# The values products of an attention head: second parts first, and all twenty in one run on TensorE

## The chip, the cores and the metric

The kernel runs on one core of one Trainium2 chip. The metric is the device time of one execution in microseconds; a kernel's time is the median of several. Work is spread over five engines, each with its own queue that is worked through in order: TensorE (PE in the profile, its weight loads PEld), VectorE (DVE), ScalarE (ACT), GpSimd (POOL) and SyncE (SP, whose queue SPq issues the transfers here).

## What is computed

A block of adaptive layer norm, attention with a compressive memory, and a token-mixing MLP, on 2048 rows of 1024 numbers. The part that matters is the attention of one head in one segment of 512 rows; there are 32 heads and 4 segments, so 128 of them:

```python
logits = jnp.einsum("bhqd,bhkd->bhqk", qs, ks) * scale + mask
p = _softmax(logits, axis=-1)
a_dot = jnp.einsum("bhqk,bhkd->bhqd", p, vs)
...
o = g * a_mem + (1.0 - g) * a_dot
```

The mask is causal. `a_mem` comes from a memory that is carried from segment to segment. After the attention follow the output projection `o @ wo`, a second layer norm and the MLP.

## The kernel before

**Stages.** First the input is normed and projected (`project(0, ...)` and what stands around it, to about 140 us of the span). Then a loop over n works through the 128 heads, numbered t*4+h, where t counts 32 steps of four heads of one group and segment. After it come the output projection (`out_proj`, sixteen blocks of 128 rows) and the MLP (`mix`, to the end).

**One pass of the loop.** Pass n traces, in this order: `scores` of head n, `maxima` of head n+3 (`LEADS`), `values` of head n-1 (`VL` = 1), and then one of the four pieces of `project` that lies 8 heads ahead (`LEADP`). Into some passes go loads of normed rows (`reload_h`), of weights (`load_w`, and for the output projection lines 503 on), and of modulation weights (`mod_late`).

**scores** (lines 372 to 393) makes the unnormalised probabilities. Four products of q and k (lines 379, 382, 385, 386) go to two PSUM banks ("s2"), ACT takes their exponentials into `p32` (lines 380, 383, 387), POOL zeroes what the mask hides in the diagonal blocks (line 390, two instructions), ACT casts the result to float16 as the first part of `ph` (line 392), and POOL subtracts to get the rest as its second part (line 393). `p32` and `ph` have two buffers each.

**values** (lines 395 to 425) multiplies the probabilities with the values. For each of the two parts of `ph` there are ten products, one for each pair of a block i of 128 query rows and a block j of keys that the mask lets through. They differ in width: products of the first part have 97 columns (a column of ones for the softmax sum, then three parts of the values), those of the second part 65. All twenty add up in one PSUM bank, `pv`, of which there is one. Then DVE takes a reciprocal (line 410), a sum over the three parts (line 412) and a scaling (line 414); POOL adds the memory's share (line 417), and after the fourth head of a step the result is transposed on TensorE (line 422), copied (line 424) and stored to `oT` (line 425), from where `out_proj` loads it (line 553, tile `otr`).

**Order.** The program is traced as above, and a planner that builds each engine's queue (`schedule_with_timeline_sim=True`) takes, at each point of its own simulated time, among the instructions that are ready the one with the best priority; unless told otherwise, that is the one traced first. A queue once built is fixed: the engine then waits at each instruction for what it needs. `tc.high_priority()` puts what is traced inside it ahead of the rest among the ready ones. Products that add up in one bank stay in traced order among themselves.

Of the kernel before, what the change touches and what calls it, by code (L numbers as in the profile page):

```python
# [27 lines left out]
NV = 97  # L28
# [14 lines left out]
def attention_and_mlp(ctx, tc, x, wq, wkv, wo, beta, w1, b1, w2, b2, c, wm_a, wm_b, out):  # L43
    nc = tc.nc
    V, A, G, T, SY = nc.vector, nc.scalar, nc.gpsimd, nc.tensor, nc.sync
# [20 lines left out]
    def bank(tag, bufs, name):  # L66
        return psum.tile([P, 512], F32, tag=tag, bufs=bufs, name=name)
# [327 lines left out]
    def values(t, h):  # L395
        pr, g, seg = its[t]
        d = st[t]
        am, ph = d["am"], d["ph", h]
        pv = bank("pv", 1, f"pv{t}_{h}").rearrange("p (a n) -> p a n", a=4)
        col = {0: lambda i: 128 * i, 1: lambda i: 512 + 128 * (i - 1), 2: lambda i: 1024 + 128 * (i - 2),  # L400
               3: lambda i: 896}
        n = 0
        for part, w in ((0, NV), (1, 65)):
            for i in range(4):
                for j in range(i + 1):
                    o = col[j](i)
                    T.matmul(pv[:, i, 0:w], ph[:, part, o:o + 128], d["vp"][:, j, h, 0:w], start=(n == 0),  # L407
                             stop=(n == 19), skip_group_check=True)
                    n += 1
        V.reciprocal(pv[:, :, 0], pv[:, :, 0])  # L410
        red = r_.tile([P, 4, 32], F32, tag="red", bufs=2, name=f"red{t}_{h}")
        V.tensor_reduce(red, pv[:, :, 1:97].rearrange("p a (c e) -> p a e c", c=3), axis=AX.X, op=ALU.add)
        ah = am[:, :, 32 * h:32 * h + 32]
        V.scalar_tensor_tensor(red if seg else ah, red, gate[:, 1, 4 * g + h:4 * g + h + 1],
                               pv[:, :, 0:1].to_broadcast([P, 4, 32]), op0=ALU.mult, op1=ALU.mult)
        if seg:
            G.tensor_tensor(ah, ah, red, op=ALU.add)
        if h < 3:
            return
        ps = bank("ms", 1, f"ops{t}")  # L420
        for i in range(4):
            T.transpose(ps[:, 128 * i:128 * i + 128], am[:, i], ident)
        ot = r_.tile([P, L], F32, tag="ot", bufs=1, name=f"ot{t}")
        A.copy(ot, ps)
        SY.dma_start(oT[g, :, L * seg:L * seg + L], ot)
        del st[t]
# [52 lines left out]
    for n in range(-LEADS, 4 * NI + VL):  # L479
        at(scores, n)  # L480
        at(maxima, n + LEADS)
        at(values, n - VL)
        m = n + LEADP
        if 0 <= m + 4 < 4 * NI:
            t = (m + 4) // 4
            if its[t][:2] not in W:
                W[its[t][:2]] = load_w(its[t][1], its[t][0])
        if m >= 8:
            at(project, m)
        if 59 <= m < 67:  # L490
            seg, ct = 2 + (m - 59) // 4, 2 * ((m - 59) % 4)
            reload_h(seg, ct)
            reload_h(seg, ct + 1)
        if m == 4 * NI - 6:
            gaw = a.tile([P, D], F32, name="gaw")
            spread(gaw, 0)
        if 4 * NI - 4 <= m < 4 * NI + 4:
            i = m - 4 * NI + 4
            nh, c2 = i // 4, 2 * (i % 4)
            r = a.tile([P, 2, 512], F32, tag="raw", bufs=2, name=f"wor{i}")  # L500
            SY.dma_start(r, wo[P * c2:P * c2 + 2 * P, 512 * nh:512 * nh + 512].rearrange("(c p) n -> p c n", p=P))
            for j in range(2):
                V.tensor_tensor(r[:, j], r[:, j], gaw[:, 512 * nh:512 * nh + 512], op=ALU.mult)
                wop[c2 + j, nh] = new_page(f"wo{c2 + j}_{nh}")
                split(wop[c2 + j, nh], r[:, j], A, V)
        if n >= ML0 and (n - ML0) % MLS == 0 and (n - ML0) // MLS < 32:
            mod_late((n - ML0) // MLS)
# [10 lines left out]
    w = cw_pool.__enter__()  # L518
# [344 lines left out]
```

## Time and profile before

| | us |
|---|---|
| median of 3 runs | 2363.02 |
| lowest and highest | 2362.68, 2367.99 |
| the profiled execution | 2363.29 |
| its span (first to last instruction) | 2361.6 |

| stage of the span | from, to us | PE busy | DVE busy | ACT busy | POOL busy |
|---|---|---|---|---|---|
| loop, start | 140 to 200 | 52.49 of 60 | 31.35 | 37.28 | 25.76 |
| loop, first half | 200 to 620 | 394.10 of 420 | 310.76 | 246.67 | 243.76 |
| loop, second half | 620 to 1016 | 395.26 of 396 | 249.42 | 248.28 | 220.01 |
| loop, last projections | 1016 to 1062 | 35.91 of 46 | 40.75 | 26.81 | 26.74 |
| loop, no projections left | 1062 to 1104 | 22.40 of 42 | 9.50 | 19.07 | 23.11 |
| output projection and MLP | 1104 to 2361 | 1246.90 of 1257 | 992.54 | 443.71 | 98.17 |

How to read the profile: it is one execution. A row of the timeline gives the start of a run of like instructions, the time from the start of the first to the end of the last, the engine, the line, the operation, the tiles written and read, the count, and in brackets how long the engine had been idle and what ended that. Products on TensorE are pipelined: one lasts 0.2 to 0.4 us, but the next starts long before it ends, so what a product costs is the distance from its start to the next one's. A row of groups ends with the time that the group kept its engine busy, the mean time of one in ns, and the idle time ahead of it.

### The profile page before, as it was taken

The page shows a single profiled execution, that of the slowest core. Times are in us where ns is not written, and L with a number is a line of the kernel's source. Part 1 is how long each engine was busy: PE and PEld are TensorE (multiplying, and loading weights), DVE is VectorE, ACT ScalarE, POOL GpSimd, SP SyncE. Part 2 cuts the span into 40 slices and gives each one's busy share as a digit, 9 for nine tenths or more (in the row PEclk, how much of TensorE's full clock was granted, in tenths as well). Part 3 has the DMA queues.
Part 4 walks back from the last instruction along what each step waited for, and adds up shares of the span by engine and source line. Part 5 has one row for each costly group of instructions (what it writes and reads, how often), then busy time and mean ns, then how long its engine had stood idle before and what let it go on. Part 6 is the DMA issues. An engine that isn't in the chain of part 4 may idle for free.

```text
span 2361.6 us, 37994 instructions
## 1 busy us (share of the span) xinstructions
PE 2230.0 (94%) x13729; PEld 1914.9 (81%) x13729; DVE 1729.5 (73%) x3889; ACT 1091.7 (46%) x1959; POOL 679.7 (29%) x667
## 2 busy tenths in 40 slices
PE   1889999998999999986999999999999999999999
PEld 1778889887899999964887888888888888888887
DVE  7655777777766665692999665598889877878787
ACT  3556656555566666663333433353334232424232
POOL 2415546557655555553000000013333000000000
PEclk9889999999999999986999999999999999999999
DMA  9563555567544444451455665366557532424234
GB/s 316 178 208 94 171 153 171 162 205 234 174 118 118 122 118 127 117 171 46 136 195 199 248 256 196 125 251 246 211 201 264 208 120 82 135 66 138 67 108 151
DMA packets 152779, 390.00 MB, mean 165 GB/s; under 512 B 17776, under 2 KB 55696, under 8 KB 143632
## 3 DMA queue, kind: packets, MB, share of 16 engines
q1 hardware_dynamic: 152592, 387.58, 50.5%
q8 instruction: 109, 1.79, 0.3%
q14 instruction: 78, 0.64, 0.1%
HBM read 224.18 MB, written 112.48 MB: 143 GB/s over the span
## 4 chain that ended last, share of the span: by engine, by line
PE 75%; DMA 10%; DVE 9%; issue 2%; ACT 2%; POOL 1%; SPq 1%; DVEq 0%; ACTq 0%; POOLq 0%
PE mx L661 36%; PE nps L270 12%; PE po L568 7%; PE qps L295 7%; PE pv L407 3%; DMA xb<-x1d 2%; DMA x1e<-xb 2%; PE a L379 1%; PE sx L357 1%; PE sz L357 1%; DMA rawv<-in_wkv_dram 1%; DMA sk<-nt 1%; DVE bU L115 1%; PE rd L329 1%; DVE xb L714 1%
## 5 line engine op out<-in xcount | busy, mean ns | idle before, releaser
L661 PE MATMUL mx<-bU,sp 128*128 128x512 f32 x2352 | 535.7, 390 | 3.8 <-DVE sp L115 1.7
L661 PEld LDWEIGHTS mx<-bU,sp 128*128 128x128 f32 x2352 | 441.0, 188 | 98.0 <-DVE sp L115 2.7
L270 PE MATMUL nps<-wv,h 128*128 128x256 f32 x3072 | 443.9, 285 | 2.9 <-POOL h L115 1.5
L661 PE MATMUL mx<-bA,sp 128*128 128x512 f32 x1764 | 432.2, 390 | 2.2 <-ACT cc L666 0.9
L112 ACT CAST sp<-wr 128x384 fp32r<-128x384 f32 (+2 forms) x408 | 217.2, 545 | 445.1 <-PE mx L661 374.2
L270 PEld LDWEIGHTS nps<-wv,h 128*128 128x128 f32 x3072 | 408.2, 190 | 7.4 <-POOL h L115 2.0
L661 PEld LDWEIGHTS mx<-bA,sp 128*128 128x128 f32 x1764 | 330.8, 188 | 72.8 <-ACT cc L666 1.5
L393 POOL TENSOR_TENSOR ph<-p,ph 128x1280 f16<-128x1280 f32 x128 | 343.0, 2680 | 137.5 <-ACT ph L392 137.2
L115 DVE TENSOR_TENSOR sp<-wr,sp 128x384 fp32r<-128x384 f32 (+2 forms) x408 | 259.1, 646 | 32.3 <-ACT sp L112 32.2
L668 DVE TENSOR_TENSOR ac<-mx,ac 128x512 f32<-128x512 f32 x280 | 189.5, 686 | 91.8 <-PE mx L661 91.2
L295 PE MATMUL qps<-h,wq 128*128 128x512 f32 x768 | 197.8, 408 | 2.0 <-DVE r L280 2.0
L392 ACT CAST ph<-p 128x1280 f16<-128x1280 f32 x128 | 161.0, 1258 | 57.2 <-POOL p L390 56.7
L358 DVE CUSTOM_DVE_ANT_0 sx<-sx,mask 128x128 f32<-128x128 f32 (+1 forms) x256 | 109.7, 429 | 99.4 <-PE sx L357 97.2
L568 PE MATMUL po<-wo,ots 128*128 128x512 f32 x768 | 177.0, 394 | 5.7 <-ACT ots L112 5.7
L390 POOL TENSOR_SCALAR_AFFINE_SELECT p<-p 128x256 f32<-128x256 f32 x256 | 122.5, 487 | 185.8 <-ACT p L383 89.5
L568 PEld LDWEIGHTS po<-wo,ots 128*128 128x128 f32 x768 | 146.0, 190 | 36.7 <-ACT ots L112 6.1
L295 PEld LDWEIGHTS qps<-h,wq 128*128 128x128 f32 x768 | 145.0, 194 | 35.3 <-issue 1.7
L407 PE MATMUL pv<-vp,ph 128*128 128x97 bf16 (+1 forms) x2560 | 152.7, 209 | 13.8 <-POOL ph L393 7.5
L661 PE MATMUL mx<-bB,sp 128*128 128x512 f32 x588 | 164.4, 389 | 0.0
L407 PEld LDWEIGHTS <-ph 128*128 128x128 f16 x2560 | 120.8, 102 | 41.1 <-issue 12.5
L661 PEld LDWEIGHTS mx<-bB,sp 128*128 128x128 f32 x588 | 110.4, 188 | 22.9
L668 DVE TENSOR_TENSOR cc<-mx,cc 128x512 f32<-128x512 f32 x140 | 94.6, 683 | 45.4 <-PE mx L661 43.2
(163 smaller groups left out, 3175.8 us busy)
## 6 DMA issues: line engine op xcount, KB each, us to landing
sk<-sg SPq DMA_DIRECT2D x384, 128.0 KB
wr<-in_w_dram SPq DMA_DIRECT2D x28, 1024.0 KB
wr<-in_w_dram SPq DMA_DIRECT2D x32, 768.0 KB
bstu<-ucd SPq DMA_DIRECT2D x28, 768.0 KB
x<-in_x_dram SPq DMA_DIRECT2D x32, 512.0 KB
wsp<-wv SPq DMA_DIRECT2D x32, 512.0 KB
rawm<-in_wm_b_dram SPq DMA_DIRECT2D x32, 512.0 KB
wv<-wsp SPq DMA_DIRECT2D x32, 512.0 KB
```

What stands on the lines that cost most here:

```text
L112: A.copy(hi, src)
L115: lo_eng.tensor_tensor(lo, src, hi.bitcast(F32), op=ALU.subtract)
L270: T.matmul(ps[:, aa], hp[k][:, j, 128 * tt:128 * tt + 128], wt[:, i, o:o + 256], start=(n == 0), stop=(n >= 6 * NK - 2), skip_group_check= ...
L295: T.matmul(ps, wt[:, i, o:o + 128], hp[k][:, j], start=(n == 0), stop=(n == 3 * NK - 1))
L358: V.tensor_tensor_reduce(o, o, mask[:, 384 - 128 * i:], 1.0, -3.0e38, op0=ALU.add, op1=ALU.max, accum_out=mx[:, h % 2, i:i + 1])
L390: G.affine_select(w, w, pattern=[[0, 2], [1, 128]], compare_op=ALU.is_ge, fill=0.0, base=0, channel_multiplier=-1)
L392: A.copy(ph[:, 0], p32)
L393: G.tensor_tensor(ph[:, 1], p32, ph[:, 0], op=ALU.subtract)
L407: T.matmul(pv[:, i, 0:w], ph[:, part, o:o + 128], d["vp"][:, j, h, 0:w], start=(n == 0), stop=(n == 19), skip_group_check=True)
L568: T.matmul(ps, os_[:, i, P * ct:P * ct + P], wop[ct, nh][:, j], start=(n == 0), stop=(n == 3 * NK - 1))
L661: T.matmul(ps, ops[q][:, i, P * k:P * k + P], b[:, j], start=(m == 0 and first), stop=(m == 3 * nk - 1), skip_group_check=True)
L668: V.tensor_tensor(d, ps, d, op=ALU.add)
```

## The change

In `values`, the loop over the parts runs over the second part (65 columns) first, then the first (97 columns), and the twenty products are traced at high priority. The product with `start` is now the first of the second part. Nothing else differs.

```diff
-        for part, w in ((0, NV), (1, 65)):
-            for i in range(4):
-                for j in range(i + 1):
-                    o = col[j](i)
-                    T.matmul(pv[:, i, 0:w], ph[:, part, o:o + 128], d["vp"][:, j, h, 0:w], start=(n == 0),
-                             stop=(n == 19), skip_group_check=True)
-                    n += 1
+        with tc.high_priority():
+            for part, w in ((1, 65), (0, NV)):
+                for i in range(4):
+                    for j in range(i + 1):
+                        o = col[j](i)
+                        T.matmul(pv[:, i, 0:w], ph[:, part, o:o + 128], d["vp"][:, j, h, 0:w], start=(n == 0),
+                                 stop=(n == 19), skip_group_check=True)
+                        n += 1
```

## The prediction

> **What bounds the kernel now.** I read the page first, then the stages of the loop, then TensorE's own order inside them. On the page TensorE is the busiest engine; the rows of weight loads are used below.
>
> ```profile
> span 2361.6 us, 37994 instructions
> ...
> PE 2230.0 (94%) x13729; PEld 1914.9 (81%) x13729; DVE 1729.5 (73%) x3889; ACT 1091.7 (46%) x1959; POOL 679.7 (29%) x667
> ...
> L270 PEld LDWEIGHTS nps<-wv,h 128*128 128x128 f32 x3072 | 408.2, 190 | 7.4 <-POOL h L115 2.0
> ...
> L407 PEld LDWEIGHTS <-ph 128*128 128x128 f16 x2560 | 120.8, 102 | 41.1 <-issue 12.5
> ```
>
> The profiled execution took 2363.29 us, 1.7 more than its span, and the median of the runs is 2363.02; I sum against the execution, which is the median within 0.3 us. The stages of the loop follow (busy us of PE, PEld, DVE, ACT, POOL with their counts, then the clock, DMA share and GB/s).
>
> ```profile
> 200.00:400.00 200.00, 193.17 (x1721) 177.89 (x1721) 146.11 (x420) 126.19 (x228) 109.18 (x110) 0.98 0.55 161
> 400.00:620.00 220.00, 200.93 (x1689) 180.91 (x1687) 164.65 (x451) 120.48 (x212) 134.58 (x121) 0.95 0.64 191
> 620.00:1016.00 396.00, 395.26 (x3535) 364.22 (x3534) 249.42 (x841) 248.28 (x440) 220.01 (x248) 1.00 0.45 123
> 1062.00:1104.00 42.00, 22.40 (x159) 15.24 (x155) 9.50 (x26) 19.07 (x28) 23.11 (x25) 0.54 0.09 29
> ```
>
> From 620 to 1016 TensorE idles for 0.7 us of 396: there every nanosecond of its queue is a nanosecond of the time. From 200 to 620 it idles for 25.9 us of 420, so a saving may vanish in a wait. From 1062 it is idle half of the time; that stage has another limit, below. After 1104 nothing is touched.
>
> **What the order on TensorE costs.** This is the engine's timeline where it never idles (first start, us, line, count).
>
> ```profile
> 621.75 0.22 PE L407 MATMUL pv<-vp,ph 128*128 128x97 bf16 x1
> ...
> 702.00 0.31 PE L407 MATMUL pv<-vp,ph 128*128 128x97 bf16 x3
> 702.13 0.48 PE L357 MATMUL sz<-sk 96*128 96x512 f32 x1
> 702.45 0.26 PE L407 MATMUL pv<-vp,ph 128*128 128x97 bf16 x2
> 702.55 0.68 PE L329 MATMUL rd<-MZ,pq 128*128 128x132 f32 x4
> 703.07 0.69 PE L407 MATMUL pv<-vp,ph 128*128 128x97 bf16 x15
> 703.60 0.48 PE L379 MATMUL a<-sk 98*128 98x512 f32 x1
> 703.91 0.34 PE L382 MATMUL a<-sk 98*128 98x384 f32 x1
> ...
> 705.38 1.34 PE L270 MATMUL nps<-wv,h 128*128 128x256 f32 x10
> 706.56 0.27 PE L363 MATMUL nmps<-ident,mx 128*8 128x128 f32 x1
> ...
> 709.45 0.29 PE L407 MATMUL pv<-vp,ph 128*128 128x65 bf16 x4
> 709.57 1.30 PE L270 MATMUL nps<-wv,h 128*128 128x256 f32 x9
> 710.71 0.23 PE L357 MATMUL sx<-sk 96*128 96x128 f32 x1
> ...
> 1012.64 0.40 PE L379 MATMUL a<-sk 98*128 98x512 f32 x1
> 1012.88 0.48 PE L407 MATMUL pv<-vp,ph 128*128 128x65 bf16 x10
> ```
>
> The twenty products of the head at 702.00 stand in three blocks, with one `sz` and four `rd` between them. What the reader is to see is the instruction right after a block. `a` of line 379 costs 0.24 us from its start to the next one's at 1012.64, and 0.31 behind a block (703.60 to 703.91). `sz`, as wide, has 0.32 behind a block (702.13 to 702.45). Ten projection products at 705.38 cost 1.18, so 0.118 each; the nine behind a block at 709.57 cost 1.14, which is 0.08 more than 9 times 0.118. Entering a block costs nothing: `a` at 1012.64 keeps its 0.24 though a block follows. So **each block costs about 0.08 us at its end**. The rows above offer a reason: a weight load of the f32 products lasts 190 ns, and the last product of a block, only some 30 to 45 ns long (the 0.13 us for three at 702.00), leaves most of it uncovered. The products themselves cost the same in any order.
>
> The Trainium skill ("TensorE: Matmul & The Clock Gate", "Step-by-step: what each phase is for") states that TensorE pulls weight loads ahead of matmuls in flight, so the next weights load during the current matmul. By that a change of kind costs nothing, the 0.08 is not there, and the sum below would lose its main term. The 0.08 of the rows disagrees with it here.
>
> **Term 1, fewer blocks.** I counted blocks (unbroken runs of line 407) in TensorE's timeline, and heads as the line's products in each stage (the first count in each row here, after TensorE's busy time with them) over twenty.
>
> ```profile
> 200.00:400.00 200.00, 28.93 (x560) 24.37 (x560) 0.98 0.55 161
> 400.00:620.00 220.00, 29.16 (x520) 23.00 (x520) 0.95 0.64 191
> 620.00:1016.00 396.00, 65.83 (x1100) 49.89 (x1100) 1.00 0.45 123
> ```
>
> From 620 to 1016 stand 149 blocks (the first at 621.75, the last at 1012.88) for 55 heads; from 200 to 400 46 for 28, from 400 to 620 53 for 26. With the change the first of the twenty needs the second part, which is made after the first, so all are ready at once, and nothing else has their priority: one block for each head. That removes 94, 18 and 27 blocks. At 0.08 us: 7.5, 1.4 and 2.2 us. The first two count whole (TensorE is 100% and 97% busy), the third by half, since idle time can take it: **-10.0 us**, with -7.5 and -11.1 as its ends.
>
> **Term 2, waits on POOL.** The ten wide products no longer go out after the cast of line 392; they queue for POOL's subtraction, 2.65 us later. In the queue everything behind them waits too: scores and maxima of the next heads, projections. Whether it does depends on how late POOL really is against the plan. One head in the steady stage:
>
> ```profile
> 698.51 2.64 POOL L393 TENSOR_TENSOR ph<-p,ph 128x1280 f16<-128x1280 f32 x1 [1.40 <-ACT ph L392]
> ```
>
> It ends at 701.15, and its head's second-part products stand inside the run of 15 that starts at 703.07, so they come over two microseconds after POOL is done. The cover is that margin: the plan lags behind the machine on POOL, and priority moves products only as far forward as the plan believes POOL to be ready. I cost the wait at 0; without the cover it is a fraction of a microsecond for each head (rival 2). The opposite end is a wait that goes, in the list of TensorE's waits from 140 to 1062 (us, times, longest):
>
> ```profile
> PE pv L407 <- ACT ph L392: 1.8, 2, 1.1
> ```
>
> These are waits on the cast, which no longer ends last. I take **-1 us**, between 0 and -1.8. On DVE the reciprocal comes at most 0.45 us later (ten products at 45 ns), with nothing behind it that TensorE needs soon. The one `pv` bank is taken later and given back 0.45 us later, where even the last heads, the fastest, are 5.16 us apart (below). No transfer is moved, and no queue of SP or POOL gets more or fewer instructions.
>
> **Term 3, the last heads.** From 1062 there are no projections to fill with (PE 22.40 of 42 us, clock 0.54), and the heads run as a chain on POOL and ACT. One turn of it, by the timeline of all engines:
>
> ```profile
> 1072.56 2.60 POOL L393 TENSOR_TENSOR ph<-p,ph 128x1280 f16<-128x1280 f32 x1
> 1075.22 0.73 PE L407 MATMUL pv<-vp,ph 128*128 128x65 bf16 x10 [1.37 <-POOL ph L393]
> 1076.25 1.26 ACT L392 CAST ph<-p 128x1280 f16<-128x1280 f32 x1
> 1076.88 0.35 DVE L414 SCALAR_TENSOR_TENSOR red<-red,gate,pv 128x128 f32<-128x128 f32 x1
> 1077.31 0.45 POOL L417 TENSOR_TENSOR am<-am,red 128x128 f32<-128x128 f32 x1 [0.41 <-DVE red L414]
> 1077.56 1.00 PE L407 MATMUL pv<-vp,ph 128*128 128x97 bf16 x10 [0.35 <-ACT ph L392]
> 1077.72 2.62 POOL L393 TENSOR_TENSOR ph<-p,ph 128x1280 f16<-128x1280 f32 x1
> ```
>
> A turn is 1077.72 less 1072.56, 5.16 us. The ten wide products (1.00 us here) move behind the narrow ones, so DVE's result and with it POOL's addition come some 0.9 us later (between 0.73 and 1.00). If that addition stays ahead of the next subtraction, each of five turns grows by 0.9 and the last head by 0.9: +5.4. If the plan lets the subtraction go first, it starts when the cast ends (1077.51) and a turn shrinks by about 0.1 instead; then only the last head's 0.9 is left: +0.4. Nearest is the second: the addition is ready a bare 0.28 us before the cast ends (1077.23 against 1077.51), less than it moves. I take **+1 us**, ends 0 and +5.5. It counts in full, since the loop's last result gates the next stage, by the chain of waits:
>
> ```profile
> 1098.83 4.52 DMA otr<-oT
> ...
> 1104.47 25.58 PE po L568 x100
> ```
>
> **Sum.** 2363.3 - 10.0 - 1 + 1 = 2353.3, so **2353 us**. Ends of the terms: 2363.3 - 11.1 - 1.8 + 0 = 2350 and 2363.3 - 7.5 + 0 + 5.5 = 2361.
>
> **Rivals.** (1) The 0.08 us isn't saved, because the instruction after the single block, or the new neighbours on TensorE, pay it in another place, or TensorE's plan waits as long anyway: then terms 2 and 3 alone are left, 2363.3 - 1 + 1, about 2363. For it: a planner's order isn't steered by this cost. Against: the cost is the same behind blocks of 3, 4 and 15 products. This is also where the skill's rule leads.
>
> (2) Slower: priority puts the block at the head of TensorE's queue while POOL is still subtracting. Its place is 400 to 620, where POOL also splits reloaded rows, and TensorE already idles 19 us. Its price: 26 heads at about 0.8 us (a third of a subtraction) is 21, and the gain there (1.1) goes: 2353.3 + 21 + 1 is about 2375. It decides once POOL runs more than the margin of 2 us behind the plan; for the steady stage the margin speaks against it.
>
> (3) More gain: a new order of the whole loop also sheds waits of maxima on DVE, by the same list:
>
> ```profile
> PE sz L357 <- DVE mx L358: 9.1, 6, 2.9
> PE sy L357 <- DVE mx L358: 6.0, 6, 2.7
> PE sx L357 <- DVE mx L358: 5.0, 10, 1.3
> ```
>
> Half of these 20.1 us would give 2343. Nothing says that they go rather than grow.
>
> (4) The change doesn't do what it says: the products still stand in two blocks a head (by count, 26 blocks fewer instead of 94 from 620, none before): 2363.3 - 3.1, with the small terms about 2360.
>
> **How the numbers follow.** Forecast 0.48, rival 1 0.16, rival 2 0.17, rival 3 0.12, rival 4 0.07. The likeliest gives 2353; its own range is 2350 to 2361. With rivals 1 and 4 inside, most of 3, and the mild part of 2, the range is **2343 to 2368**. A measurement of this kernel can tell about 0.3%, 7 us, from no change, so faster means under 2356. Faster: five sixths of the forecast and rival 3, 0.52. Slower, above 2370: rival 2, 0.17. Same: the rest, 0.31.
>
> **What would show it.** Right: in the changed profile, one unbroken row of twenty `pv` products a head (some 128 blocks, not 278), and the stage that ran from 620 to 1016 shorter by 7 us with TensorE still full. Right on term 2: TensorE's waits on POOL's `ph` outside the last heads stay under 2 us. Term 3 shows in a turn of about 5.0 us with the subtraction ahead of the addition, or 6.0 with the addition first. Wrong: blocks still broken, the 0.08 paid elsewhere, or idle rows of `pv` behind POOL from 400 to 620.

## The result, and the profile after

| | us |
|---|---|
| after, median of 4 (lowest, highest) | 2390.6 (2388.4, 2394.2) |
| before, median of 4 beside it | 2365.51 |
| ratio, 95% interval | 1.0104, 1.009 to 1.0119 |
| the profiled execution of after, its span | 2389.56, 2387.7 |

The kernel became 25 us slower where the forecast was 10 us faster. From the page of the kernel after (line 407 is line 408 there, and all lines behind it are one higher):

```profile
span 2387.7 us, 38019 instructions
...
PE 2239.8 (94%) x13729; PEld 1922.8 (81%) x13729; DVE 1745.5 (73%) x3889; ACT 1091.0 (46%) x1959; POOL 678.6 (28%) x667
```

TensorE is busy 9.8 us longer with the same 13729 products. To see where, I set the same pieces of work against each other. By stages, before: the stage from the first product of `qps` of step 17 to that of step 28 (the full stage below), the loop from 140 us to its last `pv` product, and what follows (columns as in the stages of the prediction).

```profile
628.30:939.90 311.60, 311.36 (x2795) 286.96 (x2794) 187.18 (x650) 194.36 (x343) 173.16 (x197) 1.00 0.46 123
140.00:1095.80 955.80, 899.03 (x7728) 811.25 (x7726) 640.67 (x1941) 576.90 (x1013) 538.94 (x553) 0.95 0.51 147
1095.80:2361.00 1265.20, 1248.01 (x5476) 1028.92 (x5476) 993.63 (x1683) 444.93 (x812) 98.61 (x61) 0.99 0.48 170
```

The same three pieces of the kernel after:

```profile
640.70:953.50 312.80, 308.44 (x2783) 285.78 (x2784) 193.10 (x644) 190.34 (x340) 170.58 (x197) 1.00 0.45 120
140.00:1124.70 984.70, 909.55 (x7746) 819.65 (x7744) 658.14 (x1946) 576.38 (x1015) 537.97 (x553) 0.93 0.49 142
1124.70:2387.00 1262.30, 1246.65 (x5476) 1027.99 (x5476) 994.19 (x1683) 445.17 (x812) 98.45 (x61) 0.99 0.48 170
```

All of the loss lies in the loop, which ends at 1124.7 instead of 1095.8, 28.9 us later: TensorE is busy 10.5 us longer there and idle 18.4 us longer. In the full stage its busy time fell (311.36 to 308.44), but that stage now has 4.4 us of idle time.

The products do stand together. TensorE's timeline in the kernel after:

```profile
702.02 0.27 PE L423 MATMUL ops<-ident,am 128*128 128x128 f32 x1
702.13 0.91 PE L408 MATMUL pv<-vp,ph 128*128 128x65 bf16 x20
702.88 0.51 PE L423 MATMUL ops<-ident,am 128*128 128x128 f32 x3
```

One row of twenty takes 0.75 us from its start to that of the next product. There are 127 such blocks for 278 (once two heads touch). The list of TensorE's waits after, from 140 to 1130:

```profile
PE sx L357 <- DVE mx L358: 13.5, 15, 2.7
PE pv L408 <- POOL ph L393: 11.6, 8, 2.9
PE kps L287 <- DVE r L280: 9.3, 8, 3.5
PE sz L357 <- DVE mx L358: 8.3, 11, 2.1
PE nmps L363 <- DVE tm L344: 6.2, 3, 3.7
...
PE sy L357 <- DVE mx L358: 5.1, 8, 1.8
```

Against 9.1, 6.0 and 5.0 us before for `sz`, `sy` and `sx`, the waits on row maxima went from 20.1 to 26.9 us. Over all rows of this list up to the loop's end the waits on VectorE grew from 35.6 to 47.1 us, those on POOL from 7.5 to 11.8. Here is one of the new waits, first on TensorE:

```profile
561.50 0.50 PE L357 MATMUL sz<-sk 96*128 96x512 f32 x1 [1.41 <-DVE mx L358]
565.46 1.11 PE L287 MATMUL kps<-ident,k 128*128 128x128 f32 x4 [3.46 <-DVE r L280]
```

and then on VectorE at that time:

```profile
561.50 0.17 DVE L411 RECIPROCAL pv<-pv 128x4 f32<-128x4 f32 x1
561.90 2.69 DVE L434 SCALAR_TENSOR_TENSOR rawm<-rawm,scb 128x1024 f32<-128x1024 f32 x1 [0.23 <-DMA rawm<-in_wm_b_dram]
...
564.52 0.55 DVE L413 TENSOR_REDUCE red<-pv 128x128 f32<-128x384 f32 x1
564.99 0.41 DVE L280 TENSOR_TENSOR r<-nps,vp 128x256 f32<-128x256 f32 x1
```

VectorE's queue has a multiplication of 2.69 us for the modulation, which nobody needs now, ahead of the 0.41 us subtraction that frees a projection bank. TensorE stands still for 3.46 us, until that subtraction is done (564.99 and 0.41, so 565.40). And the wait costs twice. The stages around it, with the clock in the third column from the end:

```profile
557.00:563.60 6.60, 3.60 (x40) 2.95 (x38) 3.18 (x7) 3.68 (x9) 4.20 (x3) 1.00 0.94 345
563.60:570.40 6.80, 4.94 (x14) 4.07 (x15) 6.80 (x18) 2.26 (x3) 4.33 (x5) 0.50 0.73 255
570.40:577.00 6.60, 6.60 (x52) 5.55 (x52) 5.84 (x12) 2.19 (x4) 1.58 (x2) 1.00 0.68 238
```

The granted clock falls to 0.50 for the 6.8 us from 563.60, in which TensorE works for 4.94 us at half speed; then it is back. Added up over the clock's records in the trace, from the first `qps` product of step 0 (85.4 and 85.6 us) to the loop's last `pv` product, TensorE was at half clock for 101.8 us before and 137.8 after.

### The profile page after: what moved, and what is told of

It reads as the page before. It is cut to its first block, busy times and chain, and to the rows that moved or that the text cites. A ratio compares the mean times of both kernels' runs of the same rounds, so it can differ in the third digit from the quotient of the medians.

```text
span 2387.7 us, 38019 instructions
## 1 busy us (share of the span) xinstructions
PE 2239.8 (94%) x13729; PEld 1922.8 (81%) x13729; DVE 1745.5 (73%) x3889; ACT 1091.0 (46%) x1959; POOL 678.6 (28%) x667
## 4 chain that ended last, share of the span: by engine, by line
PE 80%; DVE 9%; DMA 6%; issue 2%; ACT 2%; POOL 1%; SPq 1%; DVEq 0%; ACTq 0%; POOLq 0%
PE mx L662 42%; PE nps L270 12%; PE po L569 7%; PE qps L295 7%; PE pv L408 3%; DMA rawm<-in_wm_b_dram 1%; PE sx L357 1%; PE sz L357 1%; PE a L379 1%; DVE bU L115 1%; PE rd L329 1%; PE a L382 1%; PE sy L357 1%; DMA rawv<-in_wkv_dram 1%; POOL ph L393 1%
## 5 line engine op out<-in xcount | busy, mean ns | idle before, releaser
L295 PE MATMUL qps<-h,wq 128*128 128x512 f32 x768 | 206.0, 418 | 2.1 <-DVE r L280 1.9
L295 PEld LDWEIGHTS qps<-h,wq 128*128 128x128 f32 x768 | 151.2, 202 | 37.2 <-DVE r L280 2.6
L408 PE MATMUL pv<-vp,ph 128*128 128x65 bf16 (+1 forms) x2560 | 128.8, 209 | 13.1 <-POOL ph L393 11.6
L408 PEld LDWEIGHTS <-ph 128*128 128x128 f16 x2560 | 110.7, 103 | 25.0 <-POOL ph L393 14.8
```

The lines of the kernel that those rows point to most:

```text
L295: T.matmul(ps, wt[:, i, o:o + 128], hp[k][:, j], start=(n == 0), stop=(n == 3 * NK - 1))
```

## The experiments

The first four take the change apart: the priority alone, the order alone, the same idea by another means, and the changed kernel without its transfers' wait on SyncE.

**Priority alone** (e1):

```diff
+        with tc.high_priority():
             for part, w in ((0, NV), (1, 65)):
```

> High priority as in the change, but first parts first as before. Theory A (priority is the cause: it moves values products forward in the plan, and the waits that this exposes, on DVE's row maxima and behind the store of the result in SyncE's queue, take more than the saved switches give): about 2385 to 2395 us. Theory B (order is the cause: with the wide products held back until POOL is done, TensorE has less ready work to fill its gaps): about 2355 to 2365 us. Theory C (the loop's plan before was a lucky one, and any new plan costs about 1%): 2375 to 2395 us.

Measured: 2379.0 us, ratio 1.0058 (1.0043 to 1.0074), 200 blocks, loop end 1116.6.

**Order alone** (e2):

```diff
-        for part, w in ((0, NV), (1, 65)):
+        for part, w in ((1, 65), (0, NV)):
```

> Second parts first, no priority. Theory A: no loss, 2355 to 2366 us, with fewer blocks of values products than before and so a little faster. Theory B: the loss is here, 2385 to 2395 us. Theory C: 2375 to 2395 us.

Measured: 2366.39 us, 1.0003 (0.9993 to 1.0013), 177 blocks. The new order alone costs nothing, and the priority alone is over half of the loss, a little less than the 2385 us at which its theory began; the rest comes only with both together. It is not the new plan as such: against the kernel before, the order of work on VectorE differs at 1432 of 3889 places with the order alone, at 1456 with the priority alone and at 1539 with both, and TensorE's other work, ScalarE, GpSimd and the transfers stand in a new order in all three.

**Values traced ahead of the maxima, no priority** (e3):

```diff
         at(scores, n)
-        at(maxima, n + LEADS)
         at(values, n - VL)
+        at(maxima, n + LEADS)
```

> The kernel before, with values of head n-1 traced ahead of maxima of head n+3 in each pass of the loop: a mild preference for values on all engines, and a new plan. Theory C: 2375 to 2395 us, as any new plan. Theory A: a part of the loss, 2365 to 2380 us. Theory B: no loss, 2360 to 2367 us.

Measured: 2468.26 us, 1.0435 (1.0413 to 1.0456), far beyond what any of the three theories said. The whole of `values`, with its work on VectorE and POOL, goes ahead here, and the waits on row maxima and on the last head's result grow. In the waits of this kernel:

```profile
PE ops L422 <- DVE am L414: 16.3, 7, 5.3
PE sx L357 <- DVE mx L358: 13.9, 16, 3.0
PE sy L357 <- DVE mx L358: 12.8, 24, 1.4
```

**The changed kernel with the `oT` store on ScalarE's queue** (e4). SyncE's own waits had shown, after and then before:

```profile
SPq L426 <- ACT ot L425: 106.3, 27, 17.6
```

```profile
SPq L425 <- ACT ot L424: 37.0, 17, 12.5
```

so the store held up the loads behind it for longer.

```diff
-        SY.dma_start(oT[g, :, L * seg:L * seg + L], ot)
+        A.dma_start(oT[g, :, L * seg:L * seg + L], ot)
```

> The changed kernel, with the store of the result (oT) issued by ACT right behind the copy that it waits for, so that it holds up nothing in SyncE's queue. If SyncE's 106 us of waiting at that store is what delays the transfers behind it and so the loop: at most 2375 us. If these waits lie off the chain: 2386 to 2395 us.

Measured: 2380.77 us, 1.0073 (1.005 to 1.0097), against 1.0104, between the two theories. I took this for a third of the loss, until the control further down.

**A small preference** (e5), 30 places of the trace instead of all:

```diff
-        with tc.high_priority():
+        with tc.high_priority(offset=30):
```

> The changed kernel with a small preference (30 places in the order of tracing, about as much as scores and maxima of the same pass) in place of the highest priority. If the loss comes from values products that go ahead of scores and maxima of their own pass: 2383 to 2395 us, as with the change. If it comes from going ahead of projections of earlier passes: 2360 to 2372 us.

Measured: 2401.75 us, 1.0136 (1.0109 to 1.0164). A preference of 30 places loses as much as the full one, so the size is not what matters.

**VectorE's part of values traced later** (e6): what follows the products becomes a function `finish`, traced at the end of the pass.

```diff
+    def finish(t, h):
...
+        at(finish, n - VL)
         if n >= ML0 and (n - ML0) % MLS == 0 and (n - ML0) // MLS < 32:
```

> The changed kernel with what follows the products (reciprocal, sum, scaling, POOL's addition, transposes, store) traced at the end of the same pass, behind the projection piece, so that it yields to row maxima and to the projections' work on DVE. If the loss comes from reciprocals that stand too early in DVE's queue and hold up row maxima behind them while TensorE is late: at most 2378 us, with DVE's idle time ahead of reciprocals from step 17 to 28 down from 29 to under 20 us. If the place of the products on TensorE is the cause by itself: 2383 us or more.

Measured: 2390.23 us, 1.009 (1.007 to 1.0109). VectorE's idle time ahead of reciprocals in the full stage, 19.0 us before and 28.9 after, is 32.9 here. It did not fall, so this does not test what it was meant to, and its theory has no support.

**Another plan for both kernels** (e7 from before, e8 from after): the modulation weights begin one pass later.

```diff
-ML0 = 12
+ML0 = 13
```

> The kernel before, with the late modulation weights begun one pass later (ML0 = 13): no work is added or removed, but the loop is planned anew. If the plan of before is a lucky one: 2373 us or more. If not: 2358 to 2370 us.

> The changed kernel with ML0 = 13. If priority itself costs: at least 15 us over the kernel before with ML0 = 13, and 2380 us or more. If the loss is the accident of one plan: within 10 us of it.

Measured: e7 2371.47 us, 1.0014 (1.0003 to 1.0024); e8 2400.66 us, 1.0132 (1.0108 to 1.0156). Without the change the new plan costs some 3 us, and the change costs 29 us on top of it. So the loss is not one unlucky plan; a pair in which it all but vanishes comes further down (f4 and e4).

**Maxima ahead of values, and scores too** (e9, whose edit this is; e10 gives the scores 800 places as well; e11 has the maxima's preference with the new order and none for values):

```diff
-        with tc.high_priority():
+        with tc.high_priority(offset=400):
...
-        at(maxima, n + LEADS)
+        with tc.high_priority(offset=800):
+            at(maxima, n + LEADS)
```

> The changed kernel with a preference of 400 places for the products of values (the same queues as with the highest priority) and one of 800 for all of maxima, so that values products go ahead of scores and projections but no longer of row maxima. If the loss comes from values going ahead of maxima, the head of the chain that feeds scores three heads later: at most 2378 us. If from going ahead of scores or of projections: 2385 us or more.

> As the last, with scores at 800 places too: values products go ahead of projections only. If the chain of maxima and scores is what values hold up: at most 2370 us, near the kernel with the order alone (2366). If jumping ahead of projections costs as well: 2380 us or more.

> Second parts first, no priority for values, and 800 places for all of maxima: control for the two others. If row maxima gain by going first: 2350 to 2363 us. If the preference for maxima costs something by itself, which the two others would then carry too: 2370 us or more.

Measured: 2400.46, 2401.95 and 2398.13 us; 1.0147 (1.0115 to 1.0178), 1.0159 (1.0124 to 1.0194), 1.0125 (1.0093 to 1.0156). My theory, that the values are ahead of the maxima that feed the chain, falls: maxima with preference and values without it (e11) lose as much. Its waits:

```profile
PE sx L357 <- DMA sk<-sg: 14.5, 5, 7.7
PE pv L407 <- POOL ph L393: 12.2, 7, 2.9
PE sx L357 <- DVE mx L358: 12.0, 17, 2.0
PE sy L357 <- DVE mx L358: 11.0, 13, 4.4
```

The maxima are now also early against their loads. Whatever is preferred, TensorE meets something that is not there yet.

**The blocks joined with all queues held.** Two things were still mixed: products standing together, and a new plan for five engines. In the next kernels each traced instruction gets as its priority its place in the order of the kernel before, and each engine's queue is chained in that order. Only the twenty products of a head get adjacent places: where the last of them stood (f1), or where the first second-part product stood (f2). On the other four engines all traced work stands as before: in the traces of f1 and f2, VectorE, ScalarE and GpSimd have the order of the kernel before, instruction for instruction, and so have the 1207 transfers and TensorE without the values products. Lines are 201 higher.

```diff
+        self.tc.cur_priority = 100 + Placed.count + int(RANK[Placed.count])
...
+        for queue in Placed.queue.values():
+            queue.sort()
+            for (_, one), (_, other) in zip(queue, queue[1:]):
+                tc.add_manual_dep(nc.find_inst_by_name(other), one, behind)
```

> Every engine gets the queue that it has in the kernel before, instruction for instruction; only TensorE's products of a head are moved back to where the last of the twenty stood, so that each head is one block (127 for 278). No priority is given. Theory (the cost behind a block is real, and the change lost because its priority made another plan with more waits on VectorE and a longer half clock): the loop ends 10 to 15 us earlier than in the kernel before, ratio about 0.994 to 0.996, 2351 to 2356 us, TensorE's waits on VectorE's maxima as before or 2 us around that. Rival (the 0.08 us behind a block is paid in another place as soon as blocks are joined, and no plan can keep it): 0.999 to 1.002. Second rival (one long block is itself harmful, as it holds up what was between its parts, scores and maxima above all): 1.003 to 1.010, with more idle time of TensorE in 200 to 620.

> As the kernel with the blocks joined in the old queues, but the one block of a head stands where the first of its second-part products stood, so nine products go earlier, ahead of scores, maxima or projection products that stood between. All other queues are those of the kernel before. Theory: 0.994 to 0.998 too, a little worse than joined late at most, since moving nine products by a microsecond forward inside one plan holds up little. Rival (going ahead of earlier traced work is itself what costs the 12 to 30 us): 1.005 or more, and clearly slower than joined late.

Measured: f1 2366.83 us, 1.0009 (0.9998 to 1.002); f2 2364.59 us, 1.0000 (0.9992 to 1.0009); 127 blocks each. Neither the 25 us of loss nor the 10 us of gain is there. The full stage of f2 and TensorE's loop, then the same of f1:

```profile
631.40:938.60 307.20, 306.37 (x2795) 285.77 (x2794) 188.82 (x650) 193.76 (x342) 171.66 (x197) 1.00 0.46 125
140.00:1097.30 957.30, 895.38 (x7753) 812.33 (x7751) 642.76 (x1946) 578.21 (x1017) 536.13 (x553) 0.94 0.50 146
```

```profile
634.80:942.60 307.80, 306.97 (x2794) 286.63 (x2793) 187.70 (x650) 193.74 (x342) 171.62 (x197) 1.00 0.47 125
140.00:1101.10 961.10, 896.91 (x7750) 814.01 (x7748) 641.41 (x1946) 576.63 (x1016) 532.79 (x553) 0.94 0.50 146
```

The full stage has 311.60 us before and 307.2 and 307.8 here, 4.4 and 3.8 us less. It had 124 blocks and has 44; at the forecast's 0.08 us for each of the 80 that would be 6.4 us (the forecast's 7.5 us are for 94 blocks, from 620 to 1016). In the time of the whole kernel nothing is left of the gain.

**The store by ScalarE without the change** (f3), the control for e4, **and with the new order alone** (f4): the edit of e4 in the kernel before and in e2.

> The kernel before with the oT store issued by ScalarE. It is the control for the changed kernel with that store (1.0073 in place of 1.0104). If the 10 us that the store gave there are a loss of the change (SyncE's queue waits 106 us on it there and 37 us before), the kernel before gains a third of it at most: 0.998 to 1.000. If the store costs the same in every plan, it gains as much: 0.996.

> Second parts first without priority, with the oT store issued by ScalarE. If the two are independent: 1.000 times what the store gives the kernel before, 0.997 to 1.000. If every new plan loses some us by chance, as the maxima and scores with priority did: 1.000 to 1.005.

Measured: f3 2374.57 us, 1.0035 (1.0023 to 1.0047); f4 2378.8 us, 1.0053 (1.0038 to 1.0067). The same edit makes the kernel before 0.35% slower and the changed one 0.3% faster. So its 10 us in e4 were no price of the store as such: it made another plan. Both forecasts for f3 were too low, and f4 lies just above "some us by chance": new plans without any preference lose 0.35% and 0.53% here. And with the store on ScalarE the price of the priority is all but gone: 2378.8 us without it (f4), 2380.77 with it (e4), with intervals that overlap.

**Which part of the loop gives the gain back?** Joined as in f2, but only for heads 40 to 111 (g1) or 12 to 111 (g2), and nothing joined at all (g3). Only the list of places, `RANK`, differs from f2.

> The queues of the kernel before; the blocks are joined, early, for heads 40 to 111 alone (steps 10 to 27), where TensorE waits least. Theory (joining pays where TensorE does not wait, 4.4 us each in the second and the third stage of the kernel with all heads joined early, and is given back at the start, +5.3, and at the end, +2.6): the start and the end come back to 102.5 and 67.4 us, ratio 0.996 to 0.998, 2356 to 2361 us. Rival (the start's 5 us were a difference between two executions and not the join's): 0.998 to 1.001, with a start of 105 us or more.

> As the kernel with heads 40 to 111 joined, for heads 12 to 111 (steps 3 to 27). Theory: as that kernel, since steps 3 to 9 gained nothing with all heads joined: 0.996 to 0.998, start at 102.5 us. Rival (as there): 0.998 to 1.001.

> The queues of the kernel before on every engine, laid down in the same way as in the joined kernels, nothing joined. If laying down the queues is neutral: 0.9995 to 1.0005, with a start of 102.5 us, 278 blocks and the waits of the kernel before. If the start is 105 to 108 us here too, the start's 5 us do not come from the joining.

Measured: g1 2360.74 us, 0.9981 (0.9968 to 0.9994); g2 2363.68 us, 0.999 (0.9978 to 1.0002); g3 2366.25 us, 0.9998 (0.9988 to 1.0009). Holding the queues is neutral. In g3, with the queues of before, the full stage and the loop are:

```profile
627.60:939.10 311.50, 311.32 (x2794) 286.84 (x2793) 187.35 (x650) 193.86 (x343) 172.58 (x197) 1.00 0.45 123
140.00:1096.60 956.60, 899.85 (x7740) 811.50 (x7738) 640.76 (x1945) 576.58 (x1014) 540.39 (x553) 0.94 0.50 146
```

The full stage repeats to 0.1 us in these two executions of the same queues, so the 3.8 and 4.4 us are the join's. The start does not repeat: from the first `qps` product of step 0 to that of step 3 it took 102.5 us before, 105.4 in g3, and 107.4 in g1 where nothing is joined there. So the 5 us that f1 and f2 seemed to lose at the start are largely a difference between executions, as the rival had it, and the theory's reading of the start falls. g1 is the fastest kernel of all, and the only one whose interval ends below 1: by 5 us, less than the 0.3% named in the prediction. Its profiled execution took 2364.96 us, 4 more than its median, so its row in the next table does not show the gain.

All kernels side by side, sorted by ratio, each to the kernel before that ran beside it; waits are summed over TensorE's list from 140 us to the loop's end, and half clock from the first `qps` product of step 0 (84 to 87 us) to the loop's end:

| kernel | preference | ratio | loop ends, us | TensorE's waits, us | of them on VectorE | half clock, us |
|---|---|---|---|---|---|---|
| g1, middle joined, queues held | | 0.9981 | 1099.3 | 60.9 | 39.0 | 130.9 |
| g2, most joined, queues held | | 0.9990 | 1096.7 | 60.1 | 39.0 | 120.6 |
| g3, nothing joined, queues held | | 0.9998 | 1096.6 | 55.9 | 33.4 | 113.9 |
| before | none | 1 | 1095.8 | 55.9 | 35.6 | 101.8 |
| f2, joined early, queues held | | 1.0000 | 1097.3 | 61.0 | 36.7 | 118.7 |
| e2, order | none | 1.0003 | 1100.4 | 63.9 | 34.7 | 116.7 |
| f1, joined late, queues held | | 1.0009 | 1101.1 | 63.3 | 39.8 | 116.9 |
| e7, weights a pass later | none | 1.0014 | 1103.3 | 57.7 | 36.1 | 119.8 |
| f3, store by ScalarE | none | 1.0035 | 1105.8 | 62.7 | 41.1 | 119.4 |
| f4, order and store | none | 1.0053 | 1113.3 | 69.0 | 43.6 | 114.2 |
| e1, priority | values | 1.0058 | 1116.6 | 66.9 | 46.5 | 129.6 |
| e4, after and store | values | 1.0073 | 1114.3 | 72.6 | 46.7 | 124.6 |
| e6, after, finish late | values | 1.0090 | 1124.2 | 76.0 | 49.8 | 125.5 |
| after | values | 1.0104 | 1124.7 | 73.5 | 47.1 | 137.8 |
| e11, order, maxima | maxima | 1.0125 | 1131.0 | 77.0 | 40.6 | 123.8 |
| e8, after, weights later | values | 1.0132 | 1134.0 | 82.3 | 57.0 | 143.8 |
| e5, after, 30 places | values | 1.0136 | 1132.9 | 84.2 | 56.3 | 139.6 |
| e9, values and maxima | both | 1.0147 | 1130.8 | 76.6 | 39.6 | 134.5 |
| e10, and scores | all three | 1.0159 | 1132.1 | 75.8 | 32.5 | 131.9 |

(e3, far off, has 112.2 us of waits and 201.5 of half clock.) The nine kernels with a preference have the nine largest ratios of the table (f4, e1 and e4, next to each other, can't be told apart; e3 has no preference, but another order of tracing, and is slowest of all). TensorE's waits in those without stay at 56 to 69 us; with one they are 67 to 84. How far two executions differ is seen on g3 and the kernel before, with the same queues: the waits agree, the half clock is 113.9 against 101.8 us.

## Why the prediction was wrong

**The failed step is the assumption under the sum**, never written as a term of its own: that the priority moves only TensorE's products, and everything else stays. Terms 1 to 3 price the products, POOL's wait and the last heads. But a preference for some instructions makes new queues on all engines, and TensorE's waits in these are 17.6 us longer (55.9 to 73.5, of which 11.5 on VectorE and 4.3 on POOL), with more half clock behind them. Rival 3 had named the place, the waits on row maxima, and said that nothing shows that they go rather than grow; I priced only the going. The one slower rival that I priced was POOL (rival 2), and POOL was not it, so the range ended at 2368.

**What bounds the kernel**: right for the full stage, where a nanosecond of TensorE's queue is a nanosecond of time: with the queues held the stage got shorter by as much as TensorE's busy time in it fell (311.36 to 306.37, 5.0, less 0.6 us of new idle time).

**Term 1, blocks**: the count is right (127 for 128), and so is the cost at its place. I added the distance from each product to the next over the full stage and took off what the same form costs in the middle of a run: behind blocks 10.1 us before (124 blocks, 0.08 each), 2.6 after (44), 7.5 less, where 0.08 for each of the 80 blocks gives 6.4; from the first `qps` product to the loop's end 25.2 and 10.1. That it is also the 7.5 of the forecast is chance, since that one is for a longer stage. What was mis-sized is what is left of it. With the queues held 4.4 (f2) and 3.8 us (f1) reach the time of the stage, about two thirds of the 6.4; of the rest the trace shows some 0.6 us as idle time and 1.0 as slow restarts (products next to idle time that take longer than their form does elsewhere), and the remainder is spread over products of all kinds, unexplained. In the first half 2.5 us were forecast; there the two joined kernels show none in common that stands out from what executions differ by. So rival 1, that the 0.08 us is paid in another place, holds for about a third of the gain in the full stage, and its forecast of no change came true for the kernels with the blocks joined everywhere and the queues held (1.0000 and 1.0009).

By the rule of the Trainium skill ("TensorE: Matmul & The Clock Gate", "Step-by-step: what each phase is for") that weight loads are pulled ahead, read as the prediction read it, the full stage should not have changed; it changed by 3.8 and 4.4 us with the queues held, so the rows were right against that reading, and about two thirds right in size. Why a block costs 0.08 us at its end, an uncovered weight load or another thing, no run shows.

**Term 2, waits on POOL**: right. Of the 11.6 us in the list above all but some 0.5 us fall into the last heads, where TensorE has nothing else to do. Rival 2 did not come.

**Term 3, the last heads**: right. From the timeline of all engines after:

```profile
1106.09 2.61 POOL L393 TENSOR_TENSOR ph<-p,ph 128x1280 f16<-128x1280 f32 x1 [0.69 <-ACT ph L392]
...
1108.75 1.55 PE L408 MATMUL pv<-vp,ph 128*128 128x65 bf16 x20 [1.52 <-POOL ph L393]
1109.02 0.45 POOL L418 TENSOR_TENSOR am<-am,red 128x128 f32<-128x128 f32 x1
...
1111.11 2.61 POOL L393 TENSOR_TENSOR ph<-p,ph 128x1280 f16<-128x1280 f32 x1 [0.69 <-ACT ph L392]
```

A turn is 1111.11 less 1106.09, 5.02 us, with the subtraction ahead of the addition.

**Rival 4**: no; the products stand in one block a head. (Its 3.1 us belong to 39 blocks fewer, 149 less twice 55, and not to the 26 that it names.)

**Where the 28.9 us of the loop come from**, by the same count product by product, from the first `qps` product on: idle time +18.2, slow restarts next to idle time +6.0, other products +19, blocks -15.1, together 28.1. The half clock has a part in this, but not all. Measured against the lower quartile of their form in the full stage, the products that begin at half clock take 42.8 us too long before and 56.4 after, 13.6 more (46.2 in g3); what the products take longer at full clock is unexplained. The largest single share is `qps`, 8.8 to 16.7 us over its base, and most of it isn't the change's: against that quartile `qps` is 8.3 us too long before, 16.3 after, and 13.8 already in g3, which has the queues of before.

**What stays open** is why queues made with a preference mostly fit the machine worse. In four comparisons the preference costs 0.6 to 1.2%: e1 against the kernel before, after against e2, e8 against e7, and e11 against e2. In a fifth, e4 against f4, it costs 0.2%, which can't be told from nothing, and there the plan without it had lost 0.5% already; so plans without a preference differ among themselves by nearly as much as the smallest of these losses. Shown is that neither the products' standing together nor their going some products earlier inside held queues does it (f1, f2), and that the size of the preference and the maxima's place behind the values are not it. Such a case as at 561.50, a long instruction for later ahead of a short one for now, is what the waits look like; whether the queues would be as good as before with those long multiplications elsewhere wasn't tried, nor was TensorE's new queue with the old queues of the other engines, which would say whose queue loses the time.

## What to carry to other kernels

A scheduling priority is not a local edit: price it as a new plan for every engine, and in a kernel where five queues interlock expect the waits to grow (here TensorE's grew by 11 to 28 us). To learn what a local reordering is worth, hold all the queues as they were and move only those instructions; here that was worth some 4 us in the full stage, 5 us of the kernel's time where only the middle heads were joined, and nothing where all were. An edit that recovers time in the changed kernel alone (the store) says nothing of the cause until the same edit has been made in the kernel before.

## What the hardware showed besides

A wait much shorter than a slow stretch can bring one on. In the kernel after, in stretches of 3.4 us as the clock's records have them:

```profile
399.80:403.20 3.40, 1.75 (x28) 1.38 (x27) 3.37 (x9) 2.09 (x8) 1.85 (x2) 1.00 0.03 6
403.20:406.60 3.40, 3.40 (x13) 2.82 (x12) 3.40 (x11) 1.54 (x3) 0.00 (x0) 0.50 0.01 1
406.60:410.00 3.40, 3.40 (x17) 2.72 (x16) 0.29 (x2) 0.00 (x0) 0.00 (x0) 1.00 0.00 0
```

A single wait of 1.65 us lies in the first of them; TensorE is busy for the other 1.75 us, and the next 3.4 us go at half clock though it never idles in them. In the full stage a wait of 1.14 us (busy 2.40 of 3.4) was followed by full clock. No sharp bound shows: 1.81 of 3.41 us busy from 519.29 was followed by full clock too. The Trainium skill ("TensorE: Matmul & The Clock Gate", "HAM oscillation — how this bites in real kernels") has gaps over about 3.4 us as what costs the clock; this trace doesn't agree, half of that was enough.
